# The hidden layer's products in one level of the seven-product scheme instead of two, for eighteen of them

## The chip, the cores and the metric

The kernel runs on one core of a Trainium2 chip. What counts is the device time of one execution in microseconds; the figure is the median of three runs, and shorter is better. The profile is that of one execution.

## What is computed

Attention over pooled keys and values, and behind it a layer with a sine in its middle (the "snake" activation). All is float32.

```python
# q, k, v: (8 batches, 8 heads, 576, 64)
k_p, v_p = k, v averaged over 8 neighbours of the sequence     # 72 keys
attn = softmax(q @ k_p.T / 8)                                   # per batch and head
x = (attn @ v_p)                                                # to (4608, 512)
h = x @ w_in                                                    # (4608, 2048)
s = sin(alpha * h)
g = h + s * s / (alpha + 1e-9)
out = g @ w_out                                                 # (4608, 512)
```

## The kernel before

**Stages.** The 4608 rows of x are nine *units* of 512 rows. In the first stage (`run`, `hidden`), unit u = 0 to 8 computes g for its rows and stores it to a scratch tensor in memory (`g_bridge`, `store_g`), and beside that TensorE, VectorE, ScalarE and GpSimd work off the attention of batch u + 1, whose values are the x of the next unit. Units 7 and 8 have no attention beside them. In the second stage (`outputs`, from about 509 us) g is read back and multiplied by w_out.

**The scheme of seven products.** x @ w_in is split in 2 x 2 blocks and computed with seven block products instead of eight, from sums of the blocks of w_in (`combine_w_in`) and of x (`sums_of_x`, tile `bt`). The partial results are never added up by a separate engine where that can be helped: a PSUM bank that holds a partial sum is copied to another bank by ScalarE, and the next product is accumulated on top of it.

**Slots.** A unit has four groups J = 0 to 3 of two columns blocks of 128, and a group has seven *slots* k = 0 to 6, with products 1, 5, 6, 2, 7, 3, 4 in this order; so a unit has the slots 0 to 27. A product is four matmuls of 128 x 128 weights with 256 columns of x (`product`, line 834). Of what belongs to a group, slot by slot: the copy of b1 to b6 (k = 1), the copy of b6 to b7 and of b5 to p5 (k = 3, line 810), sines and squares on ScalarE (lines 984, 991), adds on VectorE (line 809), and, in the group behind it, the last sines (k = 0), the last squares (k = 1), `finish` with two adds (k = 2, line 1036) and `store_g` (k = 3).

**The second level.** In units 1 to 6, product 5 of groups 2 and 3 and product 1 of group 3 are not four matmuls. `inner_product` splits them again in 2 x 2 blocks and makes them with seven matmuls of 128 columns each (line 1014), in four pieces a, b, d, e that are spread over the slots around. It needs ScalarE copies (lines 1018, 1020, 1024) and a VectorE add (1029) between them, and space in banks 6 and 7. The sums of weight blocks for it are made once on GpSimd in slot 23 of unit 0 (`inner_w_in`, into a q tile), the sums of x in slot 2 of each unit (`inner_x`, into the tiles `last` and `ex`; both by `sums`, line 794). Around it, groups 2 and 3 have an order of their own: half of product 4 of group 1 is put behind product 1 of group 2, group 3 is begun in slot 19 of its unit, `finish` is done in two parts (`finish_before`, called from the middle of `turn_q` too), and the sines of group 3 wait behind the copy `order` (`behind_order`).

**What else is in the slots** is listed by `carry`: `at(slot, f)` puts a step of the attention in a slot, ahead of its product. For units 1 to 6: scores in slots 3 and 5 (line 308), `shifts`, exponentials in 8 to 10 (line 357), `norm` in 9 to 12 (lines 363 to 365), `turn` in 12 and 13 (32 x 32 transposes on VectorE into the tile `tr`, lines 491 to 501), `move` in 14 (16 DMAs from `tr` to `aM`, line 511), `turn_q` for the queries of the batch after the next in 23 and 24 (transposes into `tr`, lines 219 and 224) with 16 DMAs in 24 and 25 (line 234), `all_values` in 25 (lines 600, 613; copies to x at line 527), `k_t` in 26 (line 269), and loads of v, q and k on the sync queue.

**What sets the order.** The order on each engine is that of the program text; the engines wait for one another by semaphores that the tile framework places. A tile that is asked for again by name takes the buffer of the one before it, and waits for all that read that one. PSUM banks 0 to 4 turn in a ring: a group takes four of them, so its b1 is the b7 of two groups before. Banks 5 to 7 serve the attention.

**Queries.** Two buffers, `q0` and `q1`, each for one tile: a batch is loaded to one, turned into the other form in place, and the next batch (u + 2, in slot 7) takes it when its scores are done.

Of the kernel before, what the change touches and what calls it, by code (L numbers as in the profile page):

```python
# [19 lines left out]
P = 128  # L20
POOL = 8
TH = 256
# [18 lines left out]
class Kernel:  # L41
# [33 lines left out]
    def new_q(self, b):  # L75
        self.qm[b] = self.q_tile(b > 1)

    def q_tile(self, i):

        return self.qp.tile([P, 5 * self.H * self.D], F32, name=f"q{int(i)}")  # L80
# [6 lines left out]
    def pairs_q(self, b, tiles):  # L87

        nc = self.nc
        if 0 in tiles:  # L90
            self.raw = self.q_views(self.qm[b])
            self.qm[b] = self.q_tile(1)
        x = self.qm[b][:].rearrange("p (t h e d) -> p t e h d", t=5, e=2, d=self.D)
        for t in tiles:
            n = P if t < 4 else 64
            raw = self.raw[0][:, :, t, :] if t < 4 else self.raw[1]
            nc.scalar.copy(out=x[:n, t], in_=raw.rearrange("p (e h) d -> p e h d", e=2))
# [108 lines left out]
    def turn_q(self, b, part):  # L206
# [8 lines left out]
        if part == 0:  # L215
            for e in range(2):
# [3 lines left out]
                if e == 0:  # L220
                    self.finish_before()
# [27 lines left out]
    def attention(self, b):  # L249
# [22 lines left out]
        def q_t(i, copy=nc.scalar.copy):  # L272
# [3 lines left out]
            if b not in self.qt:  # L276
                self.qt[b] = self.qt_view(self.q_tile(0))
# [105 lines left out]
        def q_head(hp):  # L383

            if hp == 0:
                self.qt[b] = self.qt_view(self.q_tile(1))
# [203 lines left out]
        def all_values():  # L590
# [16 lines left out]
            nc.scalar.copy(out=self.sm.tile([P, 1], F32, name="order")[:], in_=rest[:, 1, 0:1])  # L607
# [7 lines left out]
            self.behind_order()  # L615
            self.behind_order = lambda: None
# [152 lines left out]
    def inner_w_in(self):  # L769

        w = self.q_tile(0)[:]
        at = 0
        for p, J0 in ((5, 2), (1, 3)):
            n = self.NJ - J0
            A = self.A[p][:].rearrange("p k (J j m) -> p k J j m", j=2, m=P)[:, :, J0:]
            L = lambda i, j: A[:, j, :, i]
            s1, s2, s3, s4 = (w[:, at + i * n * P:at + (i + 1) * n * P].rearrange("p (J m) -> p J m", m=P) for i in range(4))
            at += 4 * n * P
            self.sums(((s1, L(1, 0), L(1, 1), OP.add), (s2, s1, L(0, 0), OP.subtract), (s3, L(0, 0), L(1, 0), OP.subtract), (s4, L(0, 1), s2, OP.subtract)))
            self.W2[p] = J0, {1: L(0, 0), 2: L(0, 1), 3: s4, 4: L(1, 1), 5: s1, 6: s2, 7: s3}  # L780

    def inner_x(self, u):

        for p, x, out in ((5, self.bt[u][:, 0], self.last[:, 0:4 * P]),
                          (1, self.xT[u][:, 0:2, 0:TH], self.ex[:, 5].rearrange("p h x -> p (h x)")[:, 0:4 * P])):
            R = lambda i, j: x[:, i, j * P:(j + 1) * P]
            t1, t2, t3, t4 = (out[:, i * P:(i + 1) * P] for i in range(4))
            self.sums(((t1, R(0, 1), R(0, 0), OP.subtract), (t2, R(1, 1), t1, OP.subtract), (t3, R(1, 1), R(0, 1), OP.subtract), (t4, R(1, 0), t2, OP.subtract)))
            self.X2[p] = {1: R(0, 0), 2: R(1, 0), 3: R(1, 1), 4: t4, 5: t1, 6: t2, 7: t3}

    def sums(self, steps):

        for o, x, y, op in steps:
            self.nc.gpsimd.tensor_tensor(out=o, in0=x, in1=y, op=op)

# [10 lines left out]
    def hidden(self, u, extra):  # L806

        nc = self.nc
        add = lambda o, x, y: nc.vector.tensor_tensor(out=o, in0=x, in1=y, op=OP.add)  # L809
        copy = lambda o, x: nc.scalar.copy(out=o, in_=x)  # L810
        sin, square, early = self.sin, self.square, lambda G: G.J == (0 if G.u else 1)
        two = 0 < u < self.B - 1

        def begin(J):

            b1, b6, b5, b7 = (self.bank([P, JW, TH]) for _ in range(4))
            new = lambda n, **kw: self.hp.tile([P, 2, JW, 2, TH], F32, name=n, **kw)
            G = SimpleNamespace(u=u, J=J, b1=b1, b5=b5, b6=b6, b7=b7, g=new("h"), s=self.s,
                                p5=None, i1=None, i5=None, early=J == (0 if u else 1))
            if two and J > 1:  # L820
                G.i5 = self.inner_product(G, 5, b5, 7)
            if two and J == 3:
                G.i1 = self.inner_product(G, 1, b1, 6)
            return G

        def product(G, p, ps, start=False, part=range(4)):

            xT, bt = self.xT[G.u], self.bt[G.u]
            B = lambda i, j: xT[:, 2 * i:2 * i + 2, j * TH:(j + 1) * TH]
            x = {1: B(0, 0), 2: B(1, 0), 3: B(1, 1), 4: bt[:, 3], 5: bt[:, 0], 6: bt[:, 1], 7: bt[:, 2]}[p]  # L830
            for n in part:
                jj, kk = divmod(n, 2)
                f = G.J * JW + jj
                nc.tensor.matmul(ps[:, jj, :], self.A[p][:, kk, f * P:(f + 1) * P], x[:, kk, :],  # L834
                                 start=(start and n == 0), stop=(kk == 1), skip_group_check=True)

        def squares(Q, i):

            if i == 0 and not Q.early:
                square(Q, 0, 1)  # L840
            if i == 1:
                square(Q, 1, slice(0, 2))

        self.squares = squares
        for slot in range(7 * self.NJ):
            J, k = divmod(slot, 7)
            Q, G = self.before, self.group

            def extras():
                for f in extra[slot]:  # L850
                    f()

            if k == 0:
                Q = self.before = G
                N = self.next
                G = self.group = N or begin(J)
                self.next = None
                if G.i5 and not N:
                    G.i5.a()
                if Q and not G.i5:  # L860
                    self.last_sines(Q, 2)
                extras()
                if G.i1:
                    G.i5.b()
                    self.last_sines(Q, 0)
                else:
                    product(G, 1, G.b1, True)
                    if G.i5:
                        product(Q, 4, Q.b7, part=(2, 3))
            elif k == 1:  # L870
                if not G.i1:
                    copy(G.b6[:], G.b1[:])
                if G.i5 and not G.i1:
                    self.last_sines(Q, 0)
                elif Q and not G.i1:
                    squares(Q, 0)
                    squares(Q, 1)
                extras()
                if not G.i5:
                    product(G, 5, G.b5, True)  # L880
            elif k == 2:
                if Q and not G.i5:
                    self.finish(Q)
                if not G.i1:
                    extras()
                if G.i1:
                    product(G, 6, G.b6, part=(0, 1))
                    G.i5.d()
                    self.last_sines(Q, 1)
                    square(Q, 1, 0)  # L890
                    self.late = Q
                    extras()
                    self.finish_before()
                    product(G, 6, G.b6, part=(2, 3))
                elif G.i5:
                    product(G, 6, G.b6, part=(0, 1))
                    G.i5.b()
                    self.last_sines(Q, 1)
                    squares(Q, 0)
                    product(G, 6, G.b6, part=(2, 3))  # L900
                else:
                    product(G, 6, G.b6)
            elif k == 3:
                late = J == 0 and two
                if Q and not late and not G.i5:
                    self.store_g(Q)
                G.p5 = self.tp.tile([P, JW, TH], F32, name="p5")
                if G.i1:
                    square(Q, 1, 1)
                    squares(Q, 0)  # L910
                    extras()
                    product(G, 2, G.b1)
                    G.i5.e()
                    copy(G.p5[:], G.b5[:])
                else:
                    copy(G.b7[:], G.b6[:])
                    if G.i5:
                        squares(Q, 1)
                        G.i5.d()
                        self.finish(Q)  # L920
                        self.store_g(Q)
                    else:
                        copy(G.p5[:], G.b5[:])
                    extras()
                    product(G, 2, G.b1)
            elif k == 4:
                if G.i1:
                    copy(G.b7[:], G.b6[:])
                    self.behind_order = lambda: sin(G, 0, 0, G.b1)
                else:  # L930
# [646 lines left out]
```

## Time and profile before

| what | value |
|---|---|
| median of 3 runs | 905.09 us (904.48 to 905.52) |
| profiled execution: its time, its span | 905.09 us, 903.3 us |
| matmuls of the plain products, L834 | 1872 records (1104 + 768), 381 ns each from start to end |
| matmuls of the inner products, L1014 | 252 records, 275 ns each from start to end |
| sums for the second level on POOL, L794 | 8 in unit 0, then 8 a unit |
| first stage, second stage | to about 509 us, and from there on |

A float32 matmul stands as two records in the trace. A record's duration goes from its start to its modelled end, and the next one starts well before that end; what a matmul costs is the distance of two starts. PEld is the loading of weights, which lies beside the matmuls. "Idle before" is the time that an engine stood still ahead of a group of instructions, with what ended it. A row of stretches gives, for each engine, busy time and number of instructions in a window of the span.

### The profile page before, as it was taken

The page shows a single profiled execution, that of the slowest core. Times are in us where ns is not written, and L with a number is a line of the kernel's source. Part 1 is how long each engine was busy: PE and PEld are TensorE (multiplying, and loading weights), DVE is VectorE, ACT ScalarE, POOL GpSimd, SP SyncE. Part 2 cuts the span into 40 slices and gives each one's busy share as a digit, 9 for nine tenths or more (in the row PEclk, how much of TensorE's full clock was granted, in tenths as well). Part 3 has the DMA queues.
Part 4 walks back from the last instruction along what each step waited for, and adds up shares of the span by engine and source line. Part 5 has one row for each costly group of instructions (what it writes and reads, how often), then busy time and mean ns, then how long its engine had stood idle before and what let it go on. Part 6 is the DMA issues. An engine that isn't in the chain of part 4 may idle for free.

```text
span 903.3 us, 17940 instructions
## 1 busy us (share of the span) xinstructions
PE 895.5 (99%) x7014; PEld 816.4 (90%) x7014; DVE 677.1 (75%) x1011; ACT 448.1 (50%) x1070; POOL 210.6 (23%) x216
## 2 busy tenths in 40 slices
PE   8999999999999999999999999999999999999998
PEld 5887888888888888888888999999999999999998
DVE  7675766768577685764557799979798888889895
ACT  5696785877768778687976611111111111111111
POOL 4688452824428253430000000000000000000000
PEclk9999999999999999999999999999999999999999
DMA  9965867759577595648217346261618162534401
GB/s 254 252 200 154 214 167 199 198 158 254 146 210 188 172 239 138 180 135 302 93 66 233 99 137 206 54 197 40 223 27 228 35 193 71 172 92 125 139 15 40
DMA packets 128747, 141.13 MB, mean 156 GB/s; under 512 B 46920, under 2 KB 95704, under 8 KB 128664
## 3 DMA queue, kind: packets, MB, share of 16 engines
q1 hardware_dynamic: 125880, 137.88, 53.4%
q10 hardware_dynamic: 2784, 2.11, 0.9%
q8 instruction: 56, 0.92, 0.4%
q14 instruction: 27, 0.22, 0.1%
HBM read 75.37 MB, written 47.19 MB: 136 GB/s over the span
## 4 chain that ended last, share of the span: by engine, by line
PE 94%; DVE 2%; ACT 2%; DMA 1%; issue 0%; SPq 0%; DVEq 0%
PE PS L834 44%; PE PS L1310 41%; PE PS L1014 3%; PE PS L308 2%; PE PS L600 2%; PE PS L613 1%; DMA h<-in_v_dram 1%; DVE x L1265 1%; DMA h<-in_k_dram 1%; ACT s L991 0%; DVE s L1265 0%; ACT ex L357 0%; DVE r L1265 0%; ACT s L984 0%; PE PS L558 0%; PE PS L269 0%
## 5 line engine op out<-in xcount | busy, mean ns | idle before, releaser
L834 PE MATMUL PS<-home,a 128*128 128x256 f32 x1104 | 257.8, 381 | 1.3 <-ACT PS L810 0.8
L834 PEld LDWEIGHTS PS<-home,a 128*128 128x128 f32 x1104 | 205.3, 190 | 34.3 <-issue 5.7
L834 PE MATMUL PS<-home,as 128*128 128x256 f32 x768 | 183.0, 382 | 0.0
L834 PEld LDWEIGHTS PS<-home,as 128*128 128x128 f32 x768 | 141.6, 190 | 19.8 <-ACT PS L810 1.2
L1310 PE MATMUL PS<-s,wb 128*128 128x144 f32 x896 | 119.1, 286 | 0.0
L1360 POOL TENSOR_TENSOR cc<-cc,cb 128x576 f32<-128x576 f32 x1 | 2.0, 1980 | 501.6 <-DVE cb L1265 501.6
L1310 PEld LDWEIGHTS PS<-s,wb 128*128 128x128 f32 x896 | 113.7, 190 | 0.1
L991 ACT ACTIVATE s<-s,c 128x256 f32<-128x256 f32 (+1 forms) x228 | 113.5, 564 | 0.0
L809 DVE TENSOR_TENSOR h<-PS,p 128x512 f32<-128x512 f32 x72 | 49.1, 682 | 63.7 <-PE PS L834 35.6
L131 POOL TENSOR_TENSOR kvin<-kvin 96x768 f32<-96x768 f32 (+3 forms) x42 | 72.5, 1727 | 71.2 <-DMA kvin<-in_v_dram 69.6
L1438 ACT COPY PS<-PS 128x144 f32<-128x144 f32 x56 | 14.7, 263 | 145.0 <-PE PS L1310 138.1
L984 ACT ACTIVATE s<-h,al 128x256 f32<-128x256 f32 x144 | 65.6, 509 | 39.9 <-DVE h L809 39.9
L1310 PE MATMUL PS<-r,wb 128*128 128x144 f32 x512 | 73.3, 286 | 0.3 <-DVE r L1265 0.3
L1310 PE MATMUL PS<-s,a 128*128 128x144 f32 x512 | 73.2, 286 | 0.0
L1036 DVE TENSOR_TENSOR h<-PS,s 128x512 f32<-128x512 f32 x36 | 24.7, 687 | 59.9 <-ACT s L991 59.9
L984 ACT ACTIVATE s<-PS,al 128x256 f32<-128x256 f32 x144 | 60.1, 470 | 18.6 <-PE PS L834 17.6
L1310 PEld LDWEIGHTS PS<-r,wb 128*128 128x128 f32 x512 | 67.1, 190 | 0.5 <-DVE r L1265 0.5
L1310 PEld LDWEIGHTS PS<-s,a 128*128 128x128 f32 x512 | 67.1, 190 | 0.0
L810 ACT COPY PS<-PS 128x512 f32<-128x512 f32 x72 | 41.5, 576 | 34.9 <-PE PS L834 30.2
L1458 ACT COPY PS<-PS 128x144 f32<-128x144 f32 x56 | 14.7, 263 | 88.1 <-PE PS L1310 88.1
L1310 PE MATMUL PS<-s,we 128*128 128x144 f32 x384 | 54.9, 286 | 0.0
L1310 PE MATMUL PS<-x,wb 128*128 128x144 f32 x384 | 54.9, 286 | 0.0
(215 smaller groups left out, 1408.6 us busy)
## 6 DMA issues: line engine op xcount, KB each, us to landing
g_bridge<-h SPq DMA_DIRECT2D x72, 512.0 KB
r<-g_bridge SPq DMA_DIRECT2D x31, 1152.0 KB
out_dram<-o SPq DMA_DIRECT2D x122, 72.0 KB
kvin<-in_k_dram SPq DMA_DIRECT2D x14, 576.0 KB
q<-in_q_dram SPq DMA_DIRECT2D x7, 1024.0 KB
kvin<-in_v_dram SPq DMA_DIRECT2D x14, 512.0 KB
aM<-tr SPq DMA_DIRECT2D x54, 92.0 KB
aM<-tr SPq DMA_DIRECT2D x54, 88.0 KB
```

Source lines behind the costliest of these rows:

```text
L131: self.nc.gpsimd.tensor_tensor(out=t[..., 0:w] if w > D else out, in0=t[..., 0:w], in1=t[..., w:2 * w], op=OP.add)
L308: nc.tensor.matmul(ps[e][r0 + r:r0 + r + q.shape[-1], h, :], q[s], kb[s, hp, :], start=True, stop=True)
L600: nc.tensor.matmul(o[r:r + 64], w, x, start=start and i < 2, stop=False, skip_group_check=True)
L809: add = lambda o, x, y: nc.vector.tensor_tensor(out=o, in0=x, in1=y, op=OP.add)
L810: copy = lambda o, x: nc.scalar.copy(out=o, in_=x)
L834: nc.tensor.matmul(ps[:, jj, :], self.A[p][:, kk, f * P:(f + 1) * P], x[:, kk, :], start=(start and n == 0), stop=(kk == 1), skip_group_ch ...
L984: self.nc.scalar.activation(out=G.s[:, i, jj, j, :], in_=src[:, jj], func=AF.Sin, scale=self.al[:, f:f + 1])
L991: self.nc.scalar.activation(out=x, in_=x, func=AF.Square, scale=self.c[:, f:f + 1])
L1014: nc.tensor.matmul(o, W[m][:, G.J - J0], X[m], start=start and n == 0, stop=True, skip_group_check=True)
L1036: add = lambda o, x, y: self.nc.vector.tensor_tensor(out=o, in0=x, in1=y, op=OP.add)
L1310: nc.tensor.matmul(out, W[:, J // 2, J % 2, :], A[:, J, :], start=(start and J == 0), stop=(J == self.NJ - 1), skip_group_check=True)
L1438: nc.scalar.copy(out=x1[:, 0, :], in_=x0[:, 1, :])
```

## The change

The second level is taken out: all products of the first stage are four matmuls of 256 columns, and groups 2 and 3 of units 1 to 6 have the slots that groups 0 and 1 have. What a slot leaves to the next one is now a list, `self.left`, which runs ahead of the slot's attention steps. Going with it:

- `inner_w_in`, `inner_x`, `sums`, `inner_product`, `finish_before` and `behind_order` are gone, and the copies and adds of the second level with them.
- The queries have two buffers of one name instead of two names. The buffer that held the weight sums is free, and they are loaded a unit earlier: batch 3 in slot 14 of unit 0, then batch u + 3 in slot 7.
- `turn(1)` goes from slot 13 to 12, and the two parts of `turn_q` from slots 23 and 24 to 22 and 23. Its DMAs stay in 24 and 25.
- The store of group 2 comes ahead of those DMAs on the sync queue; it was behind them.
- The copy `order` runs on VectorE for batches from 2 on. It was on ScalarE.
- The tile `s` of the sines is asked for anew by each group; it was one tile for all.

The second stage is not touched. The instructions of the head and of units 0, 7 and 8 keep their order on PE, ScalarE and VectorE; GpSimd loses its eight sums in unit 0, and the sync queue has the added load there.

```diff
     def new_q(self, b):
-        self.qm[b] = self.q_tile(b > 1)
-
-    def q_tile(self, i):
-
-        return self.qp.tile([P, 5 * self.H * self.D], F32, name=f"q{int(i)}")
+        self.qm[b] = self.qp.tile([P, 5 * self.H * self.D], F32, name="q")
...
                 nc.vector.transpose(out=out, in_=x)
-                if e == 0:
-                    self.finish_before()
             return
...
-            nc.scalar.copy(out=self.sm.tile([P, 1], F32, name="order")[:], in_=rest[:, 1, 0:1])
+            (nc.vector.tensor_copy if b > 1 else nc.scalar.copy)(out=self.sm.tile([P, 1], F32, name="order")[:], in_=rest[:, 1, 0:1])
...
             self.vp.pop(b)
-            self.behind_order()
-            self.behind_order = lambda: None
             for hp in hps:
                 to_x(ps[hp].rearrange("p (t j) -> p j t", t=4), hp, 0, 512)
...
         for slot in range(7 * self.NJ):
             J, k = divmod(slot, 7)
...
+            for f in self.left:
+                f()
+            for f in extra[slot]:
+                f()
             if k == 0:
...
+                before = self.group
+                G = self.group = SimpleNamespace(
+                    u=u, J=J, b1=bank(), g=self.hp.tile([P, 2, JW, 2, TH], F32, name="h"),
+                    s=self.hp.tile([P, 2, JW, 2, TH], F32, name="s", bufs=1))
...
+            def left0(G=G, Q=before):
+                G.b6 = bank()
+                nc.scalar.copy(out=G.b6[:], in_=G.b1[:])
+                if Q:
+                    squares(Q)
+
+            def left1(G=G, Q=before):
+                if Q:
                     self.finish(Q)
...
+            def left2(G=G, Q=before, late=late):
+                if Q and not late:
                     self.store_g(Q)
+                G.b7 = bank()
+                nc.scalar.copy(out=G.b7[:], in_=G.b6[:])
                 G.p5 = self.tp.tile([P, JW, TH], F32, name="p5")
...
+                nc.scalar.copy(out=G.p5[:], in_=G.b5[:])
+
+            def left3(G=G):
+                sin(G, 0, 0, G.b1)
+                square(G, 0, 0)
+
+            def left4(G=G):
                 add(G.g[:, 1, :, 1], G.b7[:], G.p5[:])
...
+            def left5(G=G, Q=before, late=late):
+                if late:
                     self.store_g(Q)
                 add(G.g[:, 0, :, 1], G.b6[:], G.p5[:])
                 sin(G, 1, 1, G.g[:, 1, :, 1])
...
+                add(G.g[:, 0, :, 0], G.b1[:], G.s[:, 0, :, 0])
+
+            def left6(G=G):
+                sin(G, 0, 1, G.g[:, 0, :, 1])
+                if early(G):
+                    square(G, 0, 1)
+                sin(G, 1, 0, G.b7)
+
+            self.left = [(left0, left1, left2, left3, left4, left5, left6)[k]]
+            if k == 1:
+                G.b5 = bank()
+            p = (1, 5, 6, 2, 7, 3, 4)[k]
+            product(p, getattr(G, {1: "b1", 5: "b5", 6: "b6", 2: "b1", 7: "b7", 3: "b6", 4: "b7"}[p]), k < 2)
...
             at(9, self.load_q, 2)
-            at(23, self.inner_w_in)
+            at(14, self.load_q, 3)
...
-                at((12, 13, 13, 13)[i], A.turn, i)
+                at((12, 12, 13, 13)[i], A.turn, i)
...
-            if 2 < u + 2 <= last:
-                at(7, self.load_q, u + 2)
-            at(2, self.inner_x, u)
+            if u + 3 <= last:
+                at(7, self.load_q, u + 3)
             turn = 22
...
             for part in range(4):
-                at(((turn, turn + 1) if u == 0 else (23, 24))[part] if part < 2 else turn + part, self.turn_q, u + 2, part)
+                at(turn + part, self.turn_q, u + 2, part)
...
-                self.qp = pool(att, "qp", 1)
+                self.qp = pool(att, "qp", 2)
...
-                self.s = self.hp.tile([P, 2, JW, 2, TH], F32, name="s", bufs=1)
```

## The prediction

> **What bounds the kernel now.** I read the page first: engine shares, then the chain that ended last.
>
> ```profile
> PE 895.5 (99%) x7014; PEld 816.4 (90%) x7014; DVE 677.1 (75%) x1011; ACT 448.1 (50%) x1070; POOL 210.6 (23%) x216
> ...
> PE 94%; DVE 2%; ACT 2%; DMA 1%; issue 0%; SPq 0%; DVEq 0%
> ```
>
> TensorE is busy 99% of the span and is 94% of the chain. A busy share may hide pipelined waiting, so next I read PE's own waits. The longest that lies behind the head is one:
>
> ```profile
> PE PS L834 <- ACT PS L810: 0.8, 1, 0.8
> ```
>
> It lies at 64.0 us, in unit 0. Units 1 to 6 show no wait of PE that the view lists. So in them what PE is given to do is the time, and I count it. The stretches (us, then busy time and count of each engine):
>
> ```profile
> core 0: us, PE busy (x) PEld busy (x) DVE busy (x) ACT busy (x) POOL busy (x), PEclk, DMA share, GB/s
> 154.04:168.79 14.75, 14.75 (x68) 12.87 (x69) 11.46 (x19) 11.97 (x22) 8.58 (x6) 1.00 0.97 246
> 168.79:188.36 19.57, 19.57 (x112) 17.47 (x110) 12.59 (x25) 15.23 (x40) 11.29 (x11) 1.00 0.62 168
> ...
> 412.28:509.10 96.82, 96.82 (x449) 85.25 (x450) 60.61 (x89) 72.55 (x159) 0.00 (x0) 1.00 0.46 163
> ```
>
> The second row is unit 2 from its first inner matmul to its values (L600): the only stretch of a unit whose matmuls the change touches. The last row is units 7 and 8, one-level products alone, with the same slots as the changed kernel's. The granted clock is 1.00 in all. An fp32 matmul is two records. 96.82 us / 448 = 216.1 ns a 256-column record. The timeline of PE gives the short one:
>
> ```profile
> 181.24 0.38 PE L1014 MATMUL PS<-ex,q 128*128 128x128 f32 x2
> 181.46 0.39 PE L1014 MATMUL PS<-home,as 128*128 128x128 f32 x2
> 181.69 0.39 PE L1014 MATMUL PS<-last,q 128*128 128x128 f32 x2
> 181.91 1.03 PE L834 MATMUL PS<-home,a 128*128 128x256 f32 x4
> 182.77 0.38 PE L1014 MATMUL PS<-home,q 128*128 128x128 f32 x2
> ```
>
> Start to start, six short records take 181.91 - 181.24 = 0.67 us, 112 ns each, and four long ones 0.86. The 0.38 is latency, not cost.
>
> **PE's part.** An inner product is seven 128-column matmuls, 14 records x 112 ns = 1.57 us; the plain one is four of 256 columns, 8 x 216.1 = 1.73. The change swaps 18 (three in each of six units) back: 18 x 0.16 = +2.9 us. The window sums it with its joints. It holds 68 long and 42 short records in 19.57 us. After, it holds 68 + 24 = 92 long ones, 92 x 0.2161 = 19.88, and 0.09 for the step to L600 (that step takes 205 ns after a short record, where 112 is usual): 19.97. The difference is 0.40 a unit, 2.4 in all. It is less than 2.9 because the old window had two hesitations of PE between long records, 63 ns at 172.1 and 48 at 184.4. No such thing is in the plain stretches, so I take 2.4 and keep 2.9 as an end.
>
> The Trainium skill speaks against this: TensorE: Matmul & The Clock Gate, section Back-to-back issue gap, has the spacing of matmuls set by weight load and matmul together, with about 81 ns at 128 columns and 131 at 512. Read linearly, a 128-column record would cost 0.83 of a 256-column one, 14 of them more than 8 long ones, and taking the scheme out would save some 14 us (an estimate from that page). The rows above show 0.52, with weight loads of 190 ns each beside them; the measurement decides.
>
> **What else goes.** Per unit: 8 sums on POOL (L794, 5.9 us), 9 short copies on ACT (375 + 275 + 250 ns, three times, 2.7 us), three adds on DVE (L1029, 0.43 each). And once, inner_w_in on POOL at 80.5 to 85.2 us. None of them is waited for by PE in the views, so they give back nothing beyond the hesitations.
>
> **What moves, and what waits anew.** This decides whether 2.4 stands. J = 0 and 1 of units 1 to 6 already run the slots that J = 2 and 3 will run, without a wait, but with other attention work beside them. I follow unit 2 by hand with its durations. Slot 13 ends at 169.65 after (168.79 plus the 0.86 of product 4 that was put off); then a slot is 1.73 us.
>
> ```profile
> 166.40 0.69 DVE L809 TENSOR_TENSOR h<-PS,p 128x512 f32<-128x512 f32 x1
> 167.01 0.70 DVE L491 STREAM_TRANSPOSE tr<-ex 128x512 f32<-128x512 f32 x1
> 167.64 0.27 DVE L494 STREAM_TRANSPOSE tr<-ex 128x128 f32<-128x128 f32 x1
> 167.83 1.03 DVE L363 TENSOR_REDUCE sm<-ex 128x12 f32<-128x876 f32 x1
> 168.89 0.23 DVE L364 RECIPROCAL sm<-sm 128x12 f32<-128x12 f32 x1
> 169.03 0.63 DVE L809 TENSOR_TENSOR h<-PS,p 128x512 f32<-128x512 f32 x1
> ```
>
> - turn(1) goes a slot earlier, ahead of norm(3) and of the two adds of slot 13. Its two transposes are 0.82 us, so the add at 169.03 ends at 170.5. Then on ACT: two sines (0.91, to 171.4), two more (0.8, to 172.2), the copy into b6 (0.57, to 172.7). Product 6 wants b6 in slot 16, at 173.1. **Slack 0.4 us**, the tightest place. DVE's list ends at 173.2 as before, since its work is the same; so the moves (L511, SP, 173.15 on) stay.
> - turn_q goes from slots 23, 24 to 22, 23, and its two long transposes (1.25 us each) are ahead of all of finish() for J = 2, which stood partly between them. They write `tr`, which the moves read until their last landing, 184.8 by the trace's completion updates. So DVE waits there to 184.9 and turns until 187.3. Behind them is finish, whose squares end at 186.4 anyway; its first add frees the bank by 188.0. The values want that bank at about 189.0 (they start at 188.8). **Slack about 1 us.**
> - SP: the stores of J = 2 pass ahead of the 16 q<-tr moves and wait for finish (to about 189.5); the moves start at 190.5 instead of 189.4, 0.63 each. The first eight land by 198, the scores of slot 3 want them at 203. Hidden; the cover is 5 us.
> - The queries are loaded a unit earlier (3 issues, 1.18 MB; one more set in unit 0 at slot 14, none in unit 5). In unit 0 SP has nothing to issue from 51.8 to 63.7, and the moves to aM start at 69.0: room for some 6 us of transfer. The stores of slot 17 are behind it and nobody waits for them soon.
> - `order` goes to DVE for b > 1 and waits there for PE in slot 25. Behind it is the add of slot 26, which needs product 7, over 3 us later.
> - `s` becomes a new tile for each group, so the sines of slot 4 wait for the whole finish before them. For J = 3 that is 189.5 against 188.9 free; behind it are two sines, two squares (1.7 us) and the copies to x, which wait for the last values, at about 192.3: cover 1.1.
>
> Where such a step costs, it is at least nothing (all of it is added work or waits) and at most what DVE's late list takes off the slack: the largest single item there is 1.25 us a unit, 7.5 in all. I take nothing, the nearest rows being J = 0 and 1 of the same units; both ends stay for the range.
>
> The tail (from 509 us) has the same instructions on every engine, so it stays. The profiled execution took 905.09 us with a span of 903.3, and 905.09 is the median too. **905.1 + 2.4 = 907.5 us.**
>
> **Rivals.**
>
> - *Forecast: PE alone, +2.4 (2.0 to 3.1).* 907.5; 0.66. For it: PE's back-to-back rows. Against: the 0.4 us slack.
> - *A wait takes its place.* The copy to b6 in slot 16, or the bank of the values behind the transposes. From 0.4 us of lateness on, each unit pays the rest: 0.3 to 1 us x 6 on top, 909.3 to 913.5, middle 910.5; 0.24. For it: DVE fills 166.4 to 173.2 without a hole. Against: 9.9 us less of POOL, ACT and DVE work a unit.
> - *Not slower.* One mechanism: PE's stand of 0.97 us at 64.0 (ACT behind its exponentials in unit 0) goes, because the added load or the new tiles let ACT run otherwise there: 907.5 - 1.0 = 906.5. It decides if ACT reaches its copy at 63.3 earlier by 0.4 us or more. Against: in unit 0 all engines but SP and POOL's last eight sums have the old order; 0.08.
> - *Faster by more than 0.2%.* The 144 added records would have to cost under 187 ns each (4.2 us less than counted); no plain stretch shows that; 0.02.
> - *That it does not do what it says* doesn't arise in the count: the order of instructions shows all 252 short records gone and 144 long ones added.
>
> A difference of 0.2% (1.8 us) is about what a measurement of this kernel can tell from none: 906.9 is the border. The forecast lies above it by 0.6, and I give 8 in 100 of it to the other side: slower 0.66 x 0.92 + 0.24 = 0.85, same 0.05 + 0.08 = 0.13, faster 0.02. Range 906.6 to 910.0: below it is part of the third case, above it half of the second.
>
> **What would show it.** Right: the stretch from a unit's slot 14 to its L600 takes 0.40 us more, with no PE wait; units 7, 8 and the tail as long as now; DVE's long transposes begin at the last landing of the moves. Wrong: a PE wait on ACT (copy, slot 16) or on DVE (finish) in each unit, or another time at 64.0. A total under 906.5 would say that a 256-column record costs less than its 216 ns.

## The result, and the profile after

The changed kernel takes 908.73 us (median of 4 runs, 907.76 to 910.52) where the kernel before took 905.24 beside it (904.48 to 905.52): a ratio of 1.0042, interval 1.0025 to 1.0060. The medians lie 3.5 us apart. Its profiled execution took 908.75 us, with a span of 907.0, 3.7 more than the span before.

The page of the changed kernel: the engine shares, and the chain that ended last by engine. (PE is TensorE, DVE VectorE, ACT ScalarE, POOL GpSimd; SP is the engine that issues most DMAs.)

```profile
PE 898.6 (99%) x6906; PEld 815.2 (90%) x6906; DVE 664.4 (73%) x999; ACT 436.0 (48%) x998; POOL 171.9 (19%) x160
...
PE 94%; DVE 2%; ACT 1%; DMA 1%; SPq 1%; issue 0%; DVEq 0%; ACTq 0%
```

108 PE records are gone (7014 before), and PE is busy 3.1 us longer; every other engine has less to do, POOL by 39 us. PE is still the chain.

PE's own waits in the changed kernel (us in total, times, longest). The plain products are line 796 now:

```profile
PE PS L906 <- DVE full L1295: 1.1, 1, 1.1
PE PS L796 <- ACT PS L836: 0.8, 1, 0.8
PE PS L199 <- DMA h<-in_v_dram: 0.7, 1, 0.7
```

The wait of 0.8 us is that of unit 0 and is unchanged. That of 0.7 us for a load of v stands ahead of the first product. No wait in units 1 to 6 is listed, as before. The same stretches as before, each shifted by what the kernel is late there (the stretch ahead of slot 14 of unit 2, from there to its values, units 7 and 8):

```profile
core 0: us, PE busy (x) PEld busy (x) DVE busy (x) ACT busy (x) POOL busy (x), PEclk, DMA share, GB/s
155.18:169.92 14.74, 14.74 (x68) 12.87 (x69) 11.71 (x21) 11.96 (x22) 8.58 (x6) 1.00 0.95 242
169.92:189.88 19.96, 19.96 (x93) 17.29 (x92) 11.26 (x20) 14.39 (x31) 11.27 (x11) 1.00 0.64 170
415.91:512.73 96.82, 96.82 (x449) 85.25 (x450) 60.60 (x89) 71.89 (x157) 0.00 (x0) 1.00 0.44 157
```

The first and the last are as long as before; the second is 19.96 us against 19.57, with 92 long records in place of 68 long and 42 short ones (the two first records of the values are in the earlier count, one in this).

Where the time went shows when the start of the same landmarks is laid beside each other, changed less before (us): first plain product +0.88; values of unit 0 +0.75; then 0.38 or 0.39 for each of six units from one values step to the next, 2.31 in all; and two jumps between the first records of the values and what follows them, +0.32 in unit 2 and +0.23 in unit 4. The last product of the first stage is late by 3.63 and hardly anything changes behind it (+3.67 at the end). So **0.75 + 2.31 + 0.55 = 3.61** is the difference but for 0.02. The view of waits doesn't list the two jumps: PE's modelled record ends cover them.

The jump in unit 2, VectorE of the changed kernel (start, duration; a bracket is idle time and its releaser):

```profile
181.96 0.68 DVE L775 TENSOR_TENSOR h<-PS,s 128x512 f32<-128x512 f32 x1
187.14 2.37 DVE L215 STREAM_TRANSPOSE tr<-q 128x1024 f32<-128x1024 f32 x2 [4.50 <-DMA aM<-tr]
189.44 0.65 DVE L867 TENSOR_TENSOR h<-PS,s 128x512 f32<-128x512 f32 x1
190.01 1.20 DVE L867 TENSOR_TENSOR h<-h,s 128x1024 f32<-128x1024 f32 x1
191.14 0.69 DVE L218 STREAM_TRANSPOSE tr<-q 64x512 f32<-64x512 f32 x1
191.76 0.11 DVE L601 COPY order<-PS 128x1 f32<-128x1 f32 x1
```

and PE (values L594, their last part L607):

```profile
188.06 1.89 PE L796 MATMUL PS<-home,a 128*128 128x256 f32 x8
189.88 0.65 PE L594 MATMUL PS<-aM,vm 64*64 64x512 f32 x6
...
192.54 1.14 PE L607 MATMUL PS<-aM,vz 32*128 32x512 f32 x8
```

The transposes of the queries wait for the last landing of the moves. That came at 187.0, because one of the 16 issues on SP took 1.72 us and the others 0.54 to 0.59 (all 16 took 11.22; in unit 2 of the kernel before, 10.08). Behind the transposes comes `finish`, which frees the bank of the values at 190.09, when they had begun at 189.88, and behind that `order` at 191.76, which PE waits for before it writes the second half of `rest`, the part of the values that lies in that bank: it goes on at 191.93, 0.06 us after the end of that copy.

### The profile page after: what moved, and what is told of

Its sections match the earlier page's. It is cut to its first block, busy times and chain, and to the rows that moved or that the text cites. A ratio compares the mean times of both kernels' runs of the same rounds, so it can differ in the third digit from the quotient of the medians.

```text
span 907.0 us, 17533 instructions
## 1 busy us (share of the span) xinstructions
PE 898.6 (99%) x6906; PEld 815.2 (90%) x6906; DVE 664.4 (73%) x999; ACT 436.0 (48%) x998; POOL 171.9 (19%) x160
## 4 chain that ended last, share of the span: by engine, by line
PE 94%; DVE 2%; ACT 1%; DMA 1%; SPq 1%; issue 0%; DVEq 0%; ACTq 0%
PE PS L796 47%; PE PS L1133 40%; PE PS L302 2%; PE PS L594 2%; DMA h<-in_v_dram 1%; PE PS L607 1%; DVE s L1088 1%; DVE x L1088 1%; ACT s L809 0%; ACT s L802 0%; DVE r L1088 0%; PE PS L552 0%; PE PS L274 0%; PE PS L263 0%; PE PS L199 0%
## 5 line engine op out<-in xcount | busy, mean ns | idle before, releaser
L796 PE MATMUL PS<-home,a 128*128 128x256 f32 x1152 | 264.2, 381 | 1.3 <-ACT PS L836 0.8
L796 PEld LDWEIGHTS PS<-home,a 128*128 128x128 f32 x1152 | 216.7, 190 | 37.1 <-issue 4.6
L796 PE MATMUL PS<-home,as 128*128 128x256 f32 x864 | 200.0, 380 | 0.0
L796 PEld LDWEIGHTS PS<-home,as 128*128 128x128 f32 x864 | 162.7, 190 | 22.9 <-issue 0.8
L809 ACT ACTIVATE s<-s,c 128x256 f32<-128x256 f32 (+1 forms) x216 | 110.0, 572 | 0.0
L1133 PEld LDWEIGHTS PS<-s,we 128*128 128x128 f32 x384 | 50.3, 190 | 0.1
```

The source lines that it names most:

```text
L809: nc.scalar.activation(out=x, in_=x, func=AF.Square, scale=self.c[:, f:f + 1])
L1133: nc.tensor.matmul(out, W[:, J // 2, J % 2, :], A[:, J, :], start=(start and J == 0), stop=(J == self.NJ - 1), skip_group_check=True)
```

## The experiments

All times were taken in turn with the kernel before on the same chip, whose medians there were 905.7 to 905.9 (905.24 for the first row). "Unit 0" is what the values of unit 0 are late by in the profiled execution against the first profile of the kernel before, "a unit" is what each of units 1 to 6 adds from values to values without a jump, "jumps" is what units 1 to 6 lost beyond that, "end" is the lateness of the last product.

| run | median us | ratio, interval | unit 0 | a unit | jumps | end |
|---|---|---|---|---|---|---|
| changed | 908.73 | 1.0042, 1.0025-1.0060 | 0.75 | 0.385 | 0.55 | 3.63 |
| again | 908.74 | 1.0035, 1.0020-1.0050 | 0.06 | 0.385 | 1.23 | 3.59 |
| turn_late | 911.33 | 1.0061, 1.0046-1.0076 | 0.92 | 0.385 | 3.13 | 6.35 |
| q_late | 908.86 | 1.0034, 1.0021-1.0047 | 0.63 | 0.385 | 1.13 | 4.07 |
| seven_halves | 908.74 | 1.0026, 1.0015-1.0036 | 2.07 | -0.10 | 3.09 | 4.54 |
| order_act | 908.09 | 1.0025, 1.0015-1.0035 | 0.29 | 0.385 | 0.65 | 3.24 |
| values_as_before | 907.79 | 1.0025, 1.0017-1.0034 | -0.15 | 0.385 | 0 | 2.15 |
| seven_halves_values | 905.96 | 0.9998, 0.9990-1.0007 | 2.14 | -0.10 | 0 | 1.57 |
| turn_13 | 907.71 | 1.0019, 1.0009-1.0029 | 1.06 | 0.385 | 0 | 3.36 |
| exp_later | 917.90 | 1.0135, 1.0121-1.0149 | 14.43 | 0 | 0.21 | 14.65 |
| exp_split | 908.43 | 1.0029, 1.0019-1.0038 | 2.77 | 0 | 0 | 2.79 |
| before_a, one run | 909.18 | | 4.04 | 0 | 0 | 4.05 |
| before_b, one run | 906.09 | | 0.95 | 0 | 0 | 0.97 |

The theory at the start: PE's count costs 2.4 us; of the rest one part is a wait at the values behind the transposes, in some units, and one part is chance in the head. The rival: the earlier loads of the queries make the head and the moves late.

**again: the changed kernel once more.**

> The changed kernel once more, nothing edited. Its first profile is 3.7 us longer than that of before: 2.3 in the six units (0.385 each, as counted on PE), 0.75 from the head, where the first plain matmul starts 0.89 us later, and 0.55 from the values of units 2 and 4. Theory (count of columns): the 2.3 is there in every execution, the other 1.3 changes from one to the next; so this profile shows the six units 0.38 to 0.40 each where no wait stands, a head between 20.4 and 21.4 us, and 0 to 3 units with a wait at the values; the time is 907.3 to 909.5. Rival (the program itself slows the head): the first plain matmul starts at 21.2 to 21.4 again, and the time is 908.5 to 909.

The 0.385 a unit and a jump in unit 4 (0.65, before 0.23) came again; the one in unit 2 and the late head did not: unit 0 was late by 0.06. In its place unit 1 had 0.58 more. About half of that is PE in slot 16, standing for the copy to b6 (timelines of this run, ScalarE and then PE):

```profile
116.41 0.91 ACT L802 ACTIVATE s<-h,al 128x256 f32<-128x256 f32 x2 [1.45 <-DVE h L775]
117.22 0.81 ACT L802 ACTIVATE s<-PS,al 128x256 f32<-128x256 f32 x2
117.94 0.59 ACT L822 COPY PS<-PS 128x512 f32<-128x512 f32 x1
```

```profile
118.58 1.78 PE L796 MATMUL PS<-home,as 128*128 128x256 f32 x7 [0.16 <-ACT PS L822]
```

So PE can stand at the place with the least slack, as a rare event; that the earlier `turn(1)` is the reason is not shown. Against the 16 executions of the kernel before that ran beside it (median 905.77), the changed kernel is 3.0 us longer here by the medians, not 3.5.

**turn_late: the transposes of the queries a slot later, as they were.**

```diff
-                at(turn + part, self.turn_q, u + 2, part)
+                at(turn + part + (u > 0 and part < 2), self.turn_q, u + 2, part)
```

> The changed kernel with the two parts of turn_q in slots 23 and 24 as before, so that finish comes ahead of the long transposes on VectorE. Theory: the wait at the values of units 2 and 4 is for the bank that finish frees, and is gone in every unit; 0.55 us less than the changed kernel's first profile, so 907.3 to 908.4, and the spread of the times is smaller. Rival (the values wait for the last moves to aM themselves): the waits stay where the moves are late, and the time is that of the changed kernel.

The opposite happened: a jump of 0.63 in every one of units 1 to 5. The bank was free in time (VectorE of this run, unit 2; values from 190.67 on):

```profile
188.24 0.69 DVE L867 TENSOR_TENSOR h<-PS,s 128x512 f32<-128x512 f32 x1 [4.81 <-ACT s L809]
188.85 1.22 DVE L867 TENSOR_TENSOR h<-h,s 128x1024 f32<-128x1024 f32 x1
189.98 2.36 DVE L215 STREAM_TRANSPOSE tr<-q 128x1024 f32<-128x1024 f32 x2
192.27 0.66 DVE L218 STREAM_TRANSPOSE tr<-q 64x512 f32<-64x512 f32 x1
192.86 0.11 DVE L601 COPY order<-PS 128x1 f32<-128x1 f32 x1
```

What stands last is `order`: its VectorE copy at 192.86 comes behind all transposes, and PE, after a gap of 0.53 us between two records of the values, goes on at 193.03, 0.06 after the end of that copy. In the kernel before, `order` was on ScalarE, 1.26 us behind the start of the values in unit 2 (here 2.19). So the wait at the values has two parts, the bank and `order`, and what is ahead of both on VectorE sets it.

**q_late: the loads of the queries as before.**

```diff
-            at(14, self.load_q, 3)
...
-            if u + 3 <= last:
-                at(7, self.load_q, u + 3)
+            if 2 < u + 2 <= last:
+                at(7, self.load_q, u + 2)
```

> The changed kernel with the queries loaded when they were before: batch u + 2 in slot 7, none more in unit 0. Theory: the earlier load costs nothing; same time as the changed kernel within 0.5 us, waits at the values as often as there. Rival (the load of a megabyte more in unit 0, or the other buffer, makes DMAs late): the waits at the values or the late head go, 0.5 to 1.3 us less.

Nothing changed but the sizes of the jumps (0.23 in unit 2, 0.91 in unit 4). The earlier loads cost nothing that these runs can tell; the rival falls.

**order_act: the copy back on ScalarE, with the sines of group 3 behind it.**

```diff
-            (nc.vector.tensor_copy if b > 1 else nc.scalar.copy)(out=self.sm.tile([P, 1], F32, name="order")[:], in_=rest[:, 1, 0:1])
+            nc.scalar.copy(out=self.sm.tile([P, 1], F32, name="order")[:], in_=rest[:, 1, 0:1])
...
```

> The changed kernel with the copy `order` on ScalarE again and the first sines of group 3 behind it, as before; finish stays behind both long transposes. The last runs showed two waits of PE inside the values: for the bank that finish frees, and, when VectorE is late, for `order` itself, since the second half of `rest` is written only after it. Theory (both count): the second wait goes, the first stays where the moves to aM are late; a unit with late moves loses 0.3 to 0.5 us instead of 0.6, so 0.2 to 0.6 us less than the changed kernel in all. Rival (only the bank counts): the same as the changed kernel, 908.7.

Jumps of 0.13 and 0.52 stayed: they are the bank behind the late transposes, which came free 0.05 and 0.48 us after the values' start. In the changed kernel and in `again` the bank was free at 0.21, 0.12 and 0.54 and the jumps were 0.32, 0.23 and 0.65, 0.11 longer than that each; without `order` on VectorE they are 0.08 and 0.04 longer. So behind a late bank `order` costs 0.03 to 0.07 us more, and taking it away leaves the rest to the bank. But the bank is not the larger part by itself: wherever `order` is on VectorE, PE goes on 0.06 us after the end of that copy, and the jump is that end less about 1.67 us (both from the values' start; ends at 1.99, 2.33 and 2.30 us, jumps of 0.32, 0.65 and, in `turn_late` with the bank free, 0.63). Either wait alone is enough for most of a jump. No run frees the bank earlier and leaves `order` on VectorE. The median is 0.6 us under that of `again`, within intervals that overlap.

**values_as_before: the edit of order_act, and `finish` in two parts, the first between the two long transposes.**

```diff
                 nc.vector.transpose(out=out, in_=x)
+                if e == 0:
+                    self.finish_before()
...
```

> The same, and finish in two parts, the first between the two long transposes, as before: all of the second level's surroundings that protect the values, without the second level. Theory: no wait at the values in any unit, late moves or not; each unit is 0.38 to 0.39 us longer than in before, 2.3 in all, and the rest of the changed kernel's 3.0 to 3.5 goes: 907.4 to 908.0, ratio to before 1.0020 to 1.0027. Rival (the waits come from the moves' landing and not from the order on VectorE): the waits stay.

All jumps are gone, and what remains is PE's count alone: 0.385 six times, 2.30 from the values of unit 0 to the last product. Unit 2's stretch is that of the changed kernel, and VectorE shows why the values don't wait (this run; values from 188.98 on):

```profile
169.02:188.98 19.96, 19.96 (x93) 17.29 (x92) 11.66 (x22) 14.40 (x31) 11.49 (x12) 1.00 0.63 168
```

```profile
185.96 1.25 DVE L215 STREAM_TRANSPOSE tr<-q 128x1024 f32<-128x1024 f32 x1 [4.22 <-DMA aM<-tr]
187.13 0.65 DVE L883 TENSOR_TENSOR h<-PS,s 128x512 f32<-128x512 f32 x1
187.71 1.22 DVE L215 STREAM_TRANSPOSE tr<-q 128x1024 f32<-128x1024 f32 x1
188.85 1.19 DVE L883 TENSOR_TENSOR h<-h,s 128x1024 f32<-128x1024 f32 x1
```

The moves had a slow issue in this unit too (16 in 10.83 us), but the bank is free at 187.78, 1.2 us before the values.

**seven_halves and seven_halves_values: the PE count by itself.** Both do seven of the eight half-width matmuls in the 18 places where the second level stood; the first is put on the changed kernel, the second on `values_as_before`.

```diff
+                if 0 < u < self.B - 1 and (p == 5 and J > 1 or p == 1 and J == 3):
+                    for n in range(7):
+                        jj, kk, h = n // 4, n // 2 % 2, n % 2
...
+                    return
```

> The changed kernel with PE's count of the second level and nothing else of it: where before had an inner product, seven matmuls of 128 columns stand for the four of 256 (one of the eight quarters is left out, so these products lack a part). No copies, sums, or other order. Theory (PE's count alone): 14 records of 111 ns for 8 of 216, 0.16 to 0.17 us each, 18 times: 2.9 to 3.1 less than the changed kernel, 905.6 to 905.9, a little under what before gets from it. Rival (the order of the slots around the inner products matters, not the count): no difference, 908.7. By the second rival (short matmuls cost 0.83 of long ones): 14 us more.

> The run before with seven matmuls of 128 columns in place of four of 256 in the eighteen places (an eighth of these products is left out). With the values protected, the count of PE is to be seen in the time at last: each unit 0.49 us shorter than there, 0.10 shorter than in before, whose two hesitations are not there: 904.6 to 905.2, ratio to before 0.9990 to 0.9996. Rival (PE waits elsewhere as soon as it is faster): over 906.

In both, a unit is 0.49 us shorter than with plain products and 0.10 shorter than with the second level (18 x 0.16 = 2.9 us by the pitches, 6 x 0.49 = 2.94 measured). In the first, the forecast 905.6 to 905.9 was missed: jumps at the values took 1.18, 1.15 and 0.76 in units 1, 3 and 5 and gave all of it back. These are the units in which this kernel has the slow issue in its moves (16 in 11.22, 11.26 and 10.78 us). PE takes 0.49 us less on the way to the bank in every unit, but in units 2 and 4, with 10.08, nothing was lost. In the second no jump is left. Its forecast, 904.6 to 905.2, was missed too: the median is 1.8 us below that of `values_as_before`, where PE's count is 2.9 less. Both profiles are 2.1 late in unit 0, which the edit does not touch; whether most executions of these kernels are is not known.

The slow issue moved with PE's instructions. The kernel before, its variants and the two seven_halves kernels have it in units 1, 3 and 5, the seven profiles of kernels with plain products, `changed` among them, in 2 and 4; and `seven_halves` differs from `changed` in its matmuls alone. The DMA packets of the traces show what goes with it: 16 KB packets of the queue that the page calls `q8 instruction` (56 in the kernel before, 55 in the changed one). In units 1 to 6 of all 14 profiles, each of the 34 issues of a move over 0.9 us overlaps one, and ends 0.28 to 0.38 us after that packet's end (in unit 2 of the changed kernel the packet starts at 174.81, the issue of 1.72 us at 174.92); and each of the 35 packets that start within a move has an issue of at least 0.74 us beside it. So the change itself shifted which units have late moves. That the packet holds the issue up fits all of them; no run takes the packets away.

**turn_13: `values_as_before` with `turn(1)` in slot 13.**

```diff
-                at((12, 12, 13, 13)[i], A.turn, i)
+                at((12, 13, 13, 13)[i], A.turn, i)
```

> The kernel of values_as_before with turn(1) in slot 13 again. One execution of the changed kernel had PE wait 0.3 us in slot 16 of unit 1 for the copy to b6, the place with the least slack. Theory: with turn(1) behind the adds of slot 13 this slack is 0.8 us wider; no such wait, and a time at the lower end of values_as_before's, 907.1 to 907.9. Rival (that wait is rare): no difference, 907.8.

No jump anywhere, as in `values_as_before`; one move took 11.58 us for its 16 issues here and still cost nothing. The times are not told apart (907.71 and 907.79), and the profile of `values_as_before` had no such wait either. The rival, that the wait in slot 16 is rare, fits as well as the theory; it can't be settled with so rare an event.

**exp_later and exp_split: the wait of 0.97 us in unit 0.** The third case of the prediction had it go. Both are the kernel before, with exponentials behind the copies that PE waits for.

```diff
-                at((9, 9, 15, 15)[i], A.exp, i)
-                at((10, 10, 16, 16)[i], A.norm, i)
-                at((13, 13, 17, 19)[i], A.turn, i)
+                at((9, 9, 17, 17)[i], A.exp, i)
+                at((10, 10, 18, 18)[i], A.norm, i)
+                at((13, 13, 19, 19)[i], A.turn, i)
```

> The kernel before, with the second pair of exponentials of unit 0 in slot 17 instead of 15, behind the copies that PE waits 0.97 us for at 64.0 us, and its norms and transposes two slots later. Theory: that wait goes; if nothing behind is late, 1.0 us less than before, 904.2. Rival: the moves to aM start 2 us later and the values of unit 0 at 79.8 wait for them (they landed at 78.2), so 0.3 to 0.6 us are given back; or all of it, and the time is that of before.

It lost 12 us. The wait at 64.0 went, but the norms came on GpSimd behind the sums of weights and the pooling of keys (its product of the exponentials at 78.25, before at 64.69), the transposes behind them, and PE behind those (PE's waits of this run):

```profile
PE PS L834 <- DVE h L809: 11.9, 2, 10.4
```

In `exp_split` only the last exponential and its norm went to slot 17.

```diff
-                at((9, 9, 15, 15)[i], A.exp, i)
-                at((10, 10, 16, 16)[i], A.norm, i)
+                at((9, 9, 15, 17)[i], A.exp, i)
+                at((10, 10, 16, 17)[i], A.norm, i)
```

> The kernel before, with only the last exponential of unit 0 in slot 17, behind the copies, and its norm there too, ahead of GpSimd's sums of weights (in exp_later the norms had come behind them, and everything after waited). Theory: PE's wait of 0.97 us at 64.0 goes down to 0.1 or 0.2 and nothing behind it is late by more than the 0.8 us of slack: 0.7 to 0.9 less than before, 904.8. Rival: VectorE's transposes in unit 0 wait for GpSimd and PE for the add behind them, as some executions show at 69 us: no gain, or 0.5 us lost.

The rival was right in the time and in the engine that PE waits for: 0.8 us was gained at 64.0 and PE stood longer 5 us later (PE's timeline, the stretch around it, and VectorE ahead of that stand):

```profile
65.80 1.03 PE L834 MATMUL PS<-home,as 128*128 128x256 f32 x4
68.68 5.41 PE L834 MATMUL PS<-home,a 128*128 128x256 f32 x16 [1.85 <-DVE h L809]
```

```profile
68.00:74.00 6.00, 5.32 (x17) 4.37 (x18) 3.27 (x10) 2.07 (x5) 5.72 (x5) 0.72 0.26 77
```

```profile
65.94 0.71 DVE L491 STREAM_TRANSPOSE tr<-ex 128x512 f32<-128x512 f32 x1 [1.33 <-POOL ex L365]
...
66.77 1.02 DVE L363 TENSOR_REDUCE sm<-ex 128x12 f32<-128x876 f32 x1
67.83 0.23 DVE L364 RECIPROCAL sm<-sm 128x12 f32<-128x12 f32 x1
67.97 0.66 DVE L809 TENSOR_TENSOR h<-PS,p 128x512 f32<-128x512 f32 x1
```

GpSimd is not what held the add: the transposes start at 65.94, in the kernel before at 65.88. The norm that was moved, a reduction and a reciprocal of 1.26 us together, now stands between them and the add, which begins 1.26 us later (67.97, before 66.71). PE came 0.8 us earlier and its add 1.26 us later; with 0.2 us of slack before, that is the stand of 1.85. With a wait for GpSimd on top (1.24 us) the next add came 2.3 us later. To that comes the clock: 0.72 in this stretch, with records 427 ns apart for 3.4 us in place of 216, another 1.7 us. So the stand at 64.0 is not time to be had by itself: in the kernel before the add ends at 67.36, and a PE that is 0.8 us earlier would want it at 66.8 and stand 0.6 us there (an estimate from these rows).

**before_a and before_b: the kernel before, for the head.**

> The kernel before, unchanged, for its profile: does what lies ahead of unit 1 differ from one execution to the next there too? Theory (chance of the loads, not the change): its first plain matmul starts between 19.8 and 21.3 us, and PE may wait up to 1.5 us near 69 us. Rival (the change makes the head late): 20.4 to 20.5 us and no wait near 69, as in the first profile.

> The kernel before, unchanged, a second profile for the same question. Theory (chance of the loads): the first plain matmul starts between 19.8 and 21.3 us, not where the other profiles have it. Rival (the change makes the head late): 20.4 to 20.5 us again.

The first plain product began at 24.62 and 21.15 us (20.46 in the first profile), so later by 4.17 and 0.69, and about as much stands at the end: +4.05 and +0.97. That of `before_a` lies outside the 19.8 to 21.3 that the theory gave. It shows a granted clock of 0.61 early on, where the other profiles have 1.00 (its stretch from 10 to 20 us):

```profile
10.00:20.00 10.00, 10.00 (x121) 7.77 (x118) 7.19 (x13) 3.40 (x8) 4.20 (x6) 0.61 1.11 281
```

So the head of the unchanged kernel differs by as much as the changed kernel's +0.75, and the theory of chance holds for that. Neither showed the wait near 69 us, which turn_late, turn_13, seven_halves and seven_halves_values had (0.7 to 1.4 us, VectorE behind a GpSimd that was 0.65 to 2.1 us later than in the first profile of before). q_late, with the old loads, had none, though its GpSimd was as late as in turn_late: PE came 0.7 us later there. Nor had four profiles with the new loads. Whether the change makes it more frequent stays open.

## Why the prediction came out as it did

- **PE's count: right.** Foreseen 19.97 us for the stretch and 0.40 a unit; measured 19.96 and 0.385, 2.31 for six units. `values_as_before` shows it alone: 2.30. The two seven_halves kernels give the other side, 0.49 a unit for 21 half-width matmuls against 12 plain ones; 0.10 of that the second level lost in its joints, as the prediction read from the old hesitations.
- **The rule against the change: did not hold here.** TensorE: Matmul & The Clock Gate, section Back-to-back issue gap, would have made the changed kernel some 14 us faster, by the estimate that the prediction works out from it. A 128-column record costs 112 ns and a 256-column one 216 in these traces; the measurement decides.
- **The slack of 1 us at the bank of the values: too wide, and by a wait that was priced as the second case.** The step took the last landing of the moves from one unit, where SP issued 16 in 10.08 us. In every second unit up to unit 5 one issue takes about a microsecond longer (16 in 10.9 to 11.3 us in the three profiles of before, in 10.6 to 11.2 in the two profiles of the changed kernel), and the change moves this from units 1, 3 and 5 to 2 and 4, the unit that was read among them. There it cost 0.2 to 0.7 us, three times in four, and nothing in the other units.
- **"Behind it is only the add of slot 26": this step failed.** It asked what waits behind `order` on VectorE, and not who waits for `order` itself. PE does, in the middle of the values. `turn_late` shows it with the bank free (0.63 us a unit); in the changed kernel it is the wait that ends last in each jump, but without it the late bank would leave all but 0.03 to 0.07 us.
- **The slack of 0.4 us at the copy to b6: right as a place.** No other unit of these profiles lost time there; it was eaten once, in unit 1 of `again`, for 0.3 us.
- **The queries' loads, the store ahead of the DMAs, the new tiles `s`: nothing, as foreseen.** `q_late` shows it for the loads; the others show no wait.
- **The third case, a gain at 64.0: it did not occur,** and the rows beside `exp_split` say that some 0.6 of its 0.8 us would have been lost at the next add.
- **What the range did not name:** the head. Its lateness at the values of unit 0 was -0.15 to 2.14 in the profiles of the changed kernel and its variants, and 0, 0.95 and 4.04 in the three of the kernel before. The profile of before was an early one.

The median, 1.2 us above the forecast, is thus PE's 2.3, losses of 0.55 and 1.23 at the values and slot 16 in the two profiles, and a head that differs by execution. For those losses the medians (908.73 and 908.74 with them, 907.79 and 907.71 without) say the same, within intervals that overlap. That the time lies inside the range is in part luck: the upper end was drawn for a wait in each unit, and what came was a wait in one or two, beside a head that the sum left out.

No variant here beats the kernel before with the whole computation done. The best of the plain-product kernels (907.7) is 1.8 us behind it, interval 0.8 to 2.6.

## What to carry to other kernels

When a copy is put on another engine, ask both questions: what is queued behind it there, and who waits for its result, the engine that feeds it included. A slack read from one unit can be that of a good unit; look at the same step in all of them, and take the latest landing, before it is called cover. And a gain on PE shows only if what it runs into next, such as a bank that another engine frees, is early enough: 2.9 us of shorter matmuls came to nothing, and 1.8 of them showed once `finish` and `order` were moved.

## What the runs showed of the hardware that had not been expected

- One DMA issue in the 16 of a move takes 1.4 to 1.7 us in place of 0.6, in every second unit: units 1, 3 and 5 of the kernel before (all 16 in 11.08, 10.93 and 11.05 us), 2 and 4 of the changed one (11.22 and 10.86). It ends 0.37 or 0.38 us after a 16 KB packet of the queue `q8 instruction` in all five, and a change in the number of PE's instructions moves it to other units.
- A stand of PE of 1.85 us was followed, 1.1 us after its end, by 3.4 us at half the clock (427 ns a record, `exp_split`). The Trainium skill, TensorE: Matmul & The Clock Gate, section Part 1: The HAM clock gate (the "warmup" mystery), speaks of an idle window of some 3.4 us; here the clock fell without so long a stand, once. By the same measure stands of 0.81 us (64.0, the kernel before) and 1.35 us (69.5, `seven_halves_values`) left it at 1.00.
- The same kernel's first plain product began at 20.46, 21.15 and 24.62 us in three profiles of the kernel before, and the ends differed by about as much.
